# First loads shared by two DMA queues, an early exponential, and one low part moved ahead of two convolution pieces

## The chip, the cores and the metric

The kernel runs on one core of a Trainium2 chip. The metric is device time in microseconds (us): the median over executions of the whole program on that core. The engines are TensorE (PE in the rows, its weight loads PEld), VectorE (DVE), ScalarE (ACT), GpSimd (POOL) and SyncE (SP, which here only issues DMAs). ScalarE can issue DMAs too. A "q" behind an engine's name (SPq, ACTq) marks work of its queue, such as a DMA issue.

## What is computed

Two stages, all in fp32. A dynamic convolution over 7 taps whose weights are a softmax, then a two-layer MLP with a squared ReLU:

```
w = exp(weight_gen - max(weight_gen)); w /= sum(w) + 1e-9       # over the 7 taps, per token and head
out[b,s,h,:] = sum_k w[b,s,h,k] * x_padded[b, s+k, h,:]         # 4 x 4096 tokens, 192 features, 8 heads
h = out @ w_in                                                  # 192 -> 2048
g = s * relu(h)^2 + b
y = g @ w_out                                                   # 2048 -> 192
```

## The kernel before

The 16384 tokens are cut into 32 groups of 512. For each group the convolution runs on VectorE, on a layout of 4 feature quarters by 32 partitions: softmax, four product instructions, five additions, eight 32x32 transposes. The MLP then runs on TensorE in chunks of 128 hidden features. To keep fp32 accuracy from single-pass matmuls, each operand is split into a high part (a rounded copy, made by ScalarE) and a low part (the remainder, made by VectorE or read from a matmul result).

The order of all instructions is written out by hand (`tc.manual_schedule()`): each engine executes its instructions in the order in which the code calls them. The start of the program, about the first 90 us, is special: the weights `w_in` and `w_out` are loaded, split into high and low parts (`convert`), and used for group 0 as they become ready. After that a steady loop of 31 groups runs.

What the change and its surroundings touch, by name:

- `load(i)` loads a group's convolution weights `wg` (four DMAs, one for each feature quarter) and its tokens `xt` (four DMAs). Everything goes through SyncE's queue but for group 0, whose four `xt` DMAs go through ScalarE's.
- `load_weights(k)` loads a quarter of the MLP weights, two `convert` chunks, into the tile `r`: four large DMAs and eight small ones ("tails") of `w_in`, then two of `w_out`, one for each chunk.
- `convert(i)` is a generator of four steps: ScalarE's `Abs` of the loaded chunk (L187, needs the `w_in` DMAs and the chunk's `w_out` DMA); VectorE's L190, L194, L198; the copy to the high part `hi` (L203) with VectorE's L205 and L209; and six matmuls (L219 to L221), whose result ScalarE copies to the low part (L222).
- `run_pieces(g, a, b)` issues pieces a to b-1 of group g's convolution: 0 is the maximum and subtraction (L269, L271), 1 the exponential on ScalarE (L277), 2 the normalisation (L282 to L286), 3 to 6 the products (L300), 7 to 11 the additions (L311, L319), 12 the transposes, 13 and 14 the split into high and low, which end in four DMAs that rearrange the tile `xb` inside the on-chip memory (L355).
- `mm1_pair` (L408, L414) is the first matmul of a chunk, `relu2` (L443, L445, L449) makes `g` and its high part `gh` on ScalarE, `low_g` (L455) its low part `gl` on VectorE, `mm2_pair` (L482) the second matmul.

Each DMA signals its landing on one of eight semaphores, `DMAHW0` to `DMAHW7`. They are given out in turn over both queues, so a DMA waits, before it is issued, for the landing of the DMA eight places ahead of it. A queue that waits holds all that stands behind it.

At the start the code is:

```
load(0, nc.scalar)
constants()
load_weights(0)
load(1)
load_weights(1)
...
run_pieces(0, 0, 2)
ahead(0, 1)
run_pieces(0, 2, 7)
ahead(0, 3)
```

where `ahead(i, n)` issues the next n steps of `convert(i)`. The eight chunks of group 0 follow in a loop over i; in it, `run_pieces(1, *beside[i])` works on group 1's convolution beside them, with pieces 2 and 3 for i = 0.

Of the kernel before, what the change touches and what calls it, by code (L numbers as in the profile page):

```python
# [7 lines left out]
F32 = mybir.dt.float32  # L8
F32R = mybir.dt.float32r
U32 = mybir.dt.uint32  # L10
AF = mybir.ActivationFunctionType
# [9 lines left out]
def dynamic_conv_then_relu2_mlp(  # L21
# [24 lines left out]
    nc = tc.nc  # L46
# [3 lines left out]
    P = 128  # L50
# [39 lines left out]

    ORDER = list(range(1, NG)) + [0]

    def load(i, queue=nc.sync):

        g = ORDER[i]
        xt = xin.tile([P, J + HALO, FQ], F32, tag="x", name="xt")
        wg = xin.tile([P, J, HQ, K], F32, tag="wg", name="wg")
        t0 = g * T
        for q in range(Q):
            p = slice(q * C, (q + 1) * C)  # L100
            nc.sync.dma_start(  # L101
                out=wg[p].rearrange("c j h k -> c j (h k)"),
                in_=wgf[t0:t0 + T, q * HQ * K:(q + 1) * HQ * K].rearrange("(c j) n -> c j n", j=J),
            )
        for q in range(Q):
            p = slice(q * C, (q + 1) * C)
            f = slice(q * FQ, (q + 1) * FQ)
            if g == 0:
                nc.sync.dma_start(
                    out=xt[p, HALO:, :], in_=xf[t0:t0 + T, f].rearrange("(c j) n -> c j n", j=J)  # L110
                )
                for c0, c1 in ((1, C // 2), (C // 2, C)):
                    a = t0 + c0 * J - HALO
                    src = xf[a:a + 1, f]
                    nc.sync.dma_start(
                        out=xt[q * C + c0:q * C + c1, 0:HALO, :],
                        in_=bass.AP(src.tensor, src.offset, [[J * D, c1 - c0], [D, HALO], [1, FQ]]),
                    )
                continue
            src = xf[t0 - HALO:t0 - HALO + 1, f]  # L120
            queue.dma_start(
                out=xt[p],
                in_=bass.AP(src.tensor, src.offset, [[J * D, C], [D, J + HALO], [1, FQ]]),
            )
        xt_t[i], wg_t[i] = xt, wg
# [17 lines left out]
    raw_t = {}  # L143
# [2 lines left out]
    w_in_u = w_in.bitcast(U32)  # L146
    w_out_u = w_out.bitcast(U32)

    def load_weights(k):

        r = raw.tile([P, 2, CW, 2], U32, tag="r", name="r")
        rw = r.rearrange("p c n w -> p c (n w)")
        c0 = k * QUAD * P * 2
        for q in range(Q):
            src = w_in_u[q * FQ:q * FQ + 1, c0:c0 + 1]
            nc.sync.dma_start(
                out=rw[q * 32:(q + 1) * 32, :, CA * 2:CB * 2],
                in_=bass.AP(src.tensor, src.offset, [[F * 2, 32], [2 * P * 2, 2], [1, 2 * P * 2]]),
            )
        for q in range(Q):  # L160
            for i in range(2):
                f = (q + 2 * i) % Q * FQ + 32
                c = c0 + (1 - q // 2) * P * 2
                src = w_in_u[f:f + 1, c:c + 1]
                nc.sync.dma_start(
                    out=rw[q * 32 + i * TAIL:q * 32 + (i + 1) * TAIL, :, CB * 2:CO * 2],
                    in_=bass.AP(src.tensor, src.offset, [[F * 2, TAIL], [2 * P * 2, 2], [1, P * 2]]),
                )
        for c in range(2):
            o = (k * 2 + c) * 2 * P  # L170
            src = w_out_u[o:o + 1, 0:1]
            nc.sync.dma_start(
                out=rw[:, c, CO * 2:].rearrange("p (j n) -> p j n", j=2),
                in_=bass.AP(src.tensor, src.offset, [[D * 2, P], [P * D * 2, 2], [1, D * 2]]),
            )
        raw_t[k] = r

    def convert(i):

# [188 lines left out]
    def run_pieces(g, a, b):  # L368

        if g < NG:  # L370
            if g not in pieces_t:
                pieces_t[g] = conv_pieces(g)
            for f in pieces_t[g][a:b]:
                f()
# [77 lines left out]
    def low_g(n, p):  # L452
        sq, gh = g_t[n, p]
        gl = gp.tile([P, 2, T], F32R, tag="gl", name="gl")
        nc.vector.tensor_tensor(out=gl, in0=sq, in1=gh.bitcast(F32), op=ALU.subtract)  # L455
        g_t[n, p] = gh, gl
# [76 lines left out]

    with tc.manual_schedule():
        load(0, nc.scalar)
        constants()
        load_weights(0)
        load(1)
        load_weights(1)
        nc.sync.dma_start(out=s_sb, in_=s.partition_broadcast(P))  # L540
        nc.sync.dma_start(out=b_sb, in_=b.partition_broadcast(P))

        parts = [convert(i) for i in range(NC)]

        def ahead(i, n):
            for _ in range(n if i < NC else 0):
                next(parts[i])

        run_pieces(0, 0, 2)
        ahead(0, 1)  # L550
        run_pieces(0, 2, 7)
        ahead(0, 3)
        ahead(1, 1)
        run_pieces(0, 7, 15)

        beside = ((2, 4), (4, 5), (5, 7), (7, 8), (8, 10), (10, 12), (12, 14), (14, 15))
        for i in range(NC):
            n, p = divmod(i, 2)
            mm1_pair(n, p)
            if i == 0:  # L560
                ahead(1, 2)
                ahead(2, 1)
            relu2(n, [p], lambda: ahead(i + 1, 1))
            if i == 0:
                run_pieces(1, 0, 2)
            ahead(i + 2, 2)
            ahead(i + 3, 1)
            if i == NC - 1:
                sums = column_sums()
            if i > 0:  # L570
                mm2_pair((i - 1) // 2, (i - 1) % 2)
            run_pieces(1, *beside[i])
            low_g(n, p)
            if i == 0:
                load_weights(2)
            if i == NC - 1:
                set_bias(sums)
            if i == 1:
                load_weights(3)
            if i == 4:  # L580
                load(2)
        run_pieces(2, 0, 3)
        last = NG * NQ - 1
        for n in range(NQ, last + 1):
            g, k = divmod(n, NQ)
            if k == 0 and g + 2 < NG:
                load(g + 2)
            if k == 3:
                zeros_before(g + 2)
            mm1_quad(n)  # L590
            relu2(n)
            if n == NQ:
                mm2_pair(n - 1, 1)
            else:
                mm2_quad(n - 1)
            a = (3, 5), (5, 8), (9, 14), (0, 2)
            run_pieces(g + 1 + k // 3, *a[k])
            low_g(n, 0)
            if k == 0:
                scale(g - 1, (0, 2, 1, 3))  # L600
                store(g - 1, 0, NT)
            low_g(n, 1)
            a = (5, 5), (8, 9), (14, 15), (2, 3)
            run_pieces(g + 1 + k // 3, *a[k])

        for t in range(NT):
            mm2_pair(last, 0, [t], t == NT - 1)
            mm2_pair(last, 1, [t], t == NT - 1)
            scale(NG - 1, [t])
            store(NG - 1, t, t + 1)  # L610
# [30 lines left out]
```

## Time and profile before

| what | us |
|---|---|
| median of 3 executions (1181.53 to 1182.57) | 1181.69 |
| span of the profiled execution, first to last instruction | 1178.3 |
| TensorE busy in it | 1144.9 |
| VectorE busy | 938.2 |
| ScalarE busy | 826.4 |

The profile is of one execution. Its span is 3.4 us shorter than the median: that much of the time lies around the first and the last instruction. All starts below are counted from the span's first instruction.

### The profile page before, as it was taken

How to read it: one execution, taken by the hardware profiler on the slowest of the kernel's cores; microseconds unless marked ns; L12 is line 12 of the kernel's file. 1: busy time of each engine (PE TensorE's matmuls, PEld its weight loads, DVE VectorE, ACT ScalarE, POOL GpSimd, SP SyncE). 2: the span in 40 equal slices, each digit the busy share in tenths (PEclk: the TensorE clock that was granted, in tenths of full speed). 3: DMA queues.
4: the chain of work that ended last, by engine and by line, in shares of the span. 5: the costliest groups of instructions: out<-in, count | busy, mean ns of one | idle time of the engine just before them, and what ended most of it. 6: DMA issues, size and time to landing. Idle time of an engine off the chain costs nothing.

```text
span 1178.3 us, 29855 instructions
## 1 busy us (share of the span) xinstructions
PE 1144.9 (97%) x12672; PEld 1034.5 (88%) x12672; DVE 938.2 (80%) x1357; ACT 826.4 (70%) x889; POOL 6.1 (1%) x22
## 2 busy tenths in 40 slices
PE   2999999999999999999999999999999999999997
PEld 1678999999999999999999999999999999999997
DVE  7988887788887778887778898777788777888843
ACT  2767767777677677776776776767767677677674
POOL 0000000000000000000000000000000000000000
PEclk9999999999999999999999999999999999999999
DMA  7421222221122222122222112222112222212110
GB/s 155 117 44 28 40 46 47 32 46 27 35 46 46 39 40 37 30 40 47 46 33 46 26 36 46 46 35 44 29 37 42 47 46 33 45 26 36 24 24 14
DMA packets 175833, 50.17 MB, mean 43 GB/s; under 512 B 165076, under 2 KB 168660, under 8 KB 175700
## 3 DMA queue, kind: packets, MB, share of 16 engines
q1 hardware_dynamic: 172820, 47.73, 22.6%
q8 instruction: 99, 1.62, 0.6%
q10 hardware_dynamic: 2880, 0.54, 0.3%
q14 instruction: 34, 0.28, 0.1%
HBM read 27.26 MB, written 12.58 MB: 34 GB/s over the span
## 4 chain that ended last, share of the span: by engine, by line
PE 95%; DVE 2%; ACT 1%; DMA 1%; SPq 0%; issue 0%
PE po L500 47%; PE ph L432 43%; PE po L482 2%; PE ph L219 1%; PE ph L408 1%; DVE pr L300 1%; PE ph L414 1%; DMA r<-in_moe_w_in_dram 0%; DVE gl L455 0%; DVE pr L311 0%; ACT gh L449 0%; PE ph L246 0%; ACT r L445 0%; SPq L101 0%; DMA xb<-xb 0%
## 5 line engine op out<-in xcount | busy, mean ns | idle before, releaser
L500 PE MATMUL po<-wc,gh 64*128 64x384 f32 x3936 | 570.5, 356 | 0.0
L500 PE MATMUL po<-wc,gl 64*128 64x192 f32 x3936 | 492.8, 247 | 0.8 <-DVE gl L455 0.8
L455 DVE TENSOR_TENSOR gl<-r,gh 128x1024 fp32r<-128x1024 f32 x256 | 313.1, 1223 | 213.1 <-ACT gh L449 206.9
L443 ACT ACTIVATE r<-ph 128x1024 f32<-128x1024 f32 x256 | 249.0, 1024 | 300.0 <-PE ph L432 295.1
L500 PEld LDWEIGHTS po<-wc,gl 64*128 64x128 f32 x3936 | 375.7, 188 | 6.3 <-DVE gl L455 1.1
L500 PEld LDWEIGHTS po<-wc,gh 64*128 64x128 f32 x3936 | 368.7, 184 | 5.1
L432 PE MATMUL ph<-xa,wc 64*128 64x512 f32 x2976 | 365.6, 391 | 0.0
L432 PEld LDWEIGHTS ph<-xa,wc 64*128 64x128 f32 x2976 | 269.8, 184 | 52.9 <-issue 0.2
L449 ACT CAST gh<-r 128x1024 fp32r<-128x1024 f32 x256 | 269.2, 1052 | 7.9
L445 ACT ACTIVATE r<-r 128x1024 f32<-128x1024 f32 x256 | 270.7, 1057 | 0.3
L300 DVE TENSOR_TENSOR pr<-xt,w 128x1152 f32<-128x1152 f32 (+1 forms) x128 | 193.6, 1554 | 2.5 <-DMA r<-in_moe_w_in_dram 0.7
L432 PE MATMUL ph<-xb,wc 64*128 64x512 f32 x1488 | 190.4, 388 | 0.0
L432 PEld LDWEIGHTS ph<-xb,wc 64*128 64x128 f32 x1488 | 139.9, 184 | 30.5
L311 DVE TENSOR_TENSOR pr<-pr 128x768 f32<-128x768 f32 (+1 forms) x128 | 145.2, 1155 | 2.1
L512 DVE SCALAR_TENSOR_TENSOR u<-po,s_sb,bias 128x192 f32<-128x192 f32 x128 | 49.8, 410 | 1.6 <-PE po L482 1.6
L518 DVE SCALAR_TENSOR_TENSOR y<-po,s_sb,u 128x192 f32<-128x192 f32 x128 | 49.8, 409 | 0.1
L219 PE MATMUL ph<-r,eye_f 128*128 128x384 f32 x32 | 15.6, 570 | 18.2 <-DVE r L198 18.2
L319 DVE TENSOR_TENSOR acc<-pr 128x768 f32<-128x768 f32 x32 | 30.6, 958 | 1.1
L330 DVE STREAM_TRANSPOSE xT<-acc 128x128 f32<-128x128 f32 x128 | 28.5, 280 | 1.1
L335 DVE STREAM_TRANSPOSE xT<-acc 128x128 f32<-128x128 f32 x128 | 27.2, 271 | 0.0
L482 PE MATMUL po<-wc,gh 128*128 128x384 f32 x80 | 23.9, 361 | 0.1
L219 PEld LDWEIGHTS ph<-r,eye_f 128*128 128x128 f32 x32 | 5.7, 205 | 20.8 <-issue 20.8
(45 smaller groups left out, 336.0 us busy)
## 6 DMA issues: line engine op xcount, KB each, us to landing
xt<-in_x_dram SPq DMA_DIRECT2D x120, 132.0 KB, 3.4
out_dram<-y SPq DMA_DIRECT2D x128, 96.0 KB, 1.9
xb<-xb SPq DMA_DIRECT2D x128, 64.0 KB
wg<-in_weight_gen_dram SPq DMA_DIRECT2D x128, 28.0 KB, 2.6
r<-in_moe_w_out_dram SPq DMA_DIRECT2D x8, 384.0 KB, 3.7
r<-in_moe_w_in_dram SPq DMA_DIRECT2D x16, 128.0 KB, 3.0
r<-in_moe_w_in_dram SPq DMA_DIRECT2D x32, 32.0 KB, 2.2
xt<-in_x_dram ACTq DMA_DIRECT2D x4, 132.0 KB, 4.0
```

The lines of the kernel that those rows point to most:

```text
L219: nc.tensor.matmul(out=o, lhsT=eye_f, rhs=fv[:, c], start=True, stop=False)
L300: nc.vector.tensor_tensor(out=pr[:, k0:k1, :, h * G:(h + 1) * G], in0=bass.AP(xs.tensor, xs.offset, [xs.ap[0], [FQ, n], [FQ, J], [1, G]]), ...
L311: nc.vector.tensor_tensor(out=pr[:, o:o + n], in0=pr[:, o:o + n], in1=pr[:, a:a + n], op=ALU.add)
L432: nc.tensor.matmul(out=h_t[n, p][:, j], lhsT=w1(2 * k + p, part, block, j, rows), rhs=v[rows], start=(at < 2 and c == 0), stop=(at >= 4 an ...
L443: nc.scalar.activation(out=r[p], in_=h_t.pop((n, p)), func=AF.Relu)
L445: nc.scalar.activation(out=r[p], in_=r[p], func=AF.Square)
L449: nc.scalar.copy(out=gh, in_=r[p])
L455: nc.vector.tensor_tensor(out=gl, in0=sq, in1=gh.bitcast(F32), op=ALU.subtract)
L482: nc.tensor.matmul(**m)
L500: nc.tensor.matmul(**m)
L512: nc.vector.scalar_tensor_tensor(out=u[i], in0=o_t[g][tiles[i]][:, 1, :], scalar=s_sb, in1=bias, op0=ALU.mult, op1=ALU.add,)
L518: nc.vector.scalar_tensor_tensor(out=y[:, t], in0=o_t[g][t][:, 0, :], scalar=s_sb, in1=u[i - 1], op0=ALU.mult, op1=ALU.add,)
```

## The change

Three things. First, the DMAs of group 0 are shared: quarters 0 and 1 of `wg` and of `xt` go through SyncE's queue, quarters 2 and 3 through ScalarE's, and of the first `load_weights` the second tail of each pair goes through ScalarE's queue, behind group 0's exponential (for this, pieces 0 and 1 are now called ahead of `load_weights(0)`). Second, an exponential of one column of a constant tile is issued on ScalarE right after its first DMAs. Third, for the first chunk (i = 0) `low_g` comes ahead of `run_pieces(1, 2, 4)`.

```
-    def load(i, queue=nc.sync):
+    def load(i, side=nc.sync):
         g = ORDER[i]
+        queues = [nc.sync, nc.sync, side, side]
...
-            nc.sync.dma_start(
+            queues[q].dma_start(
                 out=wg[p].rearrange("c j h k -> c j (h k)"),
...
-            queue.dma_start(
+            queues[q].dma_start(
                 out=xt[p],
...
-    def load_weights(k):
+    def load_weights(k, side=nc.sync):
...
-                nc.sync.dma_start(
+                (nc.sync, side)[i].dma_start(
                     out=rw[q * 32 + i * TAIL:q * 32 + (i + 1) * TAIL, :, CB * 2:CO * 2],
...
         load(0, nc.scalar)
         constants()
-        load_weights(0)
+        warm = const.tile([P, 1], F32, name="warm")
+        nc.scalar.activation(out=warm, in_=ones_f[:, 0:1], func=AF.Exp)
+        run_pieces(0, 0, 2)
+        load_weights(0, nc.scalar)
         load(1)
...
-        run_pieces(0, 0, 2)
         ahead(0, 1)
...
+            if i == 0:
+                low_g(n, p)
             run_pieces(1, *beside[i])
-            low_g(n, p)
+            if i > 0:
+                low_g(n, p)
```

The changed file has one or more lines ahead of these places, so its line numbers are 1 to 6 higher.

On ScalarE, at the start of the program, the rows of the kernel before (with the semaphores that each waits for; `xt` and `wg` are group 0's, `r` the first weights):

```order
L121 DMA xt<-in_x_dram 32x22x48 x2
L121 DMA xt<-in_x_dram 32x22x48 [waits DMAHW1_49]
L121 DMA xt<-in_x_dram 32x22x48 [waits DMAHW4_49]
L277 ACT_TABLE_LOAD
L277 ACTIVATE e<-e 128x224 [waits DVE_49]
L187 ACTIVATE t<-r 128x768 [waits DMAHW4_49,DMAHW5_49,DMAHW3_49,DMAHW6_49,DMAHW2_49,DMAHW7_49,DMAHW1_49,DMAHW0_49]
```

And the same place of the changed kernel:

```order
L102 DMA wg<-in_weight_gen_dram 32x16x14 x2
L122 DMA xt<-in_x_dram 32x22x48 x2
L539 ACT_TABLE_LOAD
L539 ACTIVATE warm<-ones_f 128x1 [waits Pool_49]
L278 ACTIVATE e<-e 128x224 [waits DVE_49]
L167 DMA r<-in_moe_w_in_dram 16x2x256 [waits DMAHW2_49]
L167 DMA r<-in_moe_w_in_dram 16x2x256 [waits DMAHW3_49]
L167 DMA r<-in_moe_w_in_dram 16x2x256 [waits DMAHW5_49]
L167 DMA r<-in_moe_w_in_dram 16x2x256 [waits DMAHW6_49]
L188 ACTIVATE t<-r 128x768 [waits DMAHW4_49,DMAHW5_49,DMAHW3_49,DMAHW6_49,DMAHW2_49,DMAHW7_49,DMAHW1_49,DMAHW0_49]
```

The table load that belongs to the exponential now stands with the early one, none of the first four DMAs waits, and four tails stand behind the exponential.

On SyncE's queue, the start of the program in the kernel before (without the semaphores):

```order
L101 DMA wg<-in_weight_gen_dram 32x16x14 x4
L156 DMA r<-in_moe_w_in_dram 32x2x512 x4
L165 DMA r<-in_moe_w_in_dram 16x2x256 x8
L172 DMA r<-in_moe_w_out_dram 128x2x384 x2
L101 DMA wg<-in_weight_gen_dram 32x16x14 x4
```

And in the changed kernel, with the semaphores. In the order in which they are given out, the two queues alternate over the first eight (ScalarE's `wg`, SyncE's `wg`, and so on: 0 to 3 are `wg`, 4 and 6 ScalarE's `xt`, 5 and 7 SyncE's `xt`):

```order
L102 DMA wg<-in_weight_gen_dram 32x16x14 x2
L122 DMA xt<-in_x_dram 32x22x48 x2
L158 DMA r<-in_moe_w_in_dram 32x2x512 [waits DMAHW0_49]
L158 DMA r<-in_moe_w_in_dram 32x2x512 [waits DMAHW1_49]
L158 DMA r<-in_moe_w_in_dram 32x2x512 [waits DMAHW4_49]
L158 DMA r<-in_moe_w_in_dram 32x2x512 [waits DMAHW7_49]
L167 DMA r<-in_moe_w_in_dram 16x2x256 [waits DMAHW0_49]
L167 DMA r<-in_moe_w_in_dram 16x2x256 [waits DMAHW1_49]
L167 DMA r<-in_moe_w_in_dram 16x2x256 [waits DMAHW2_49]
L167 DMA r<-in_moe_w_in_dram 16x2x256 [waits DMAHW3_49]
L174 DMA r<-in_moe_w_out_dram 128x2x384 [waits DMAHW4_49]
L174 DMA r<-in_moe_w_out_dram 128x2x384 [waits DMAHW5_49]
```

The first `w_out` DMA was the 17th on this queue and is now the 13th. The third and fourth large `w_in` DMAs now stand behind the landing of `xt` DMAs, and the third and fourth tail behind that of ScalarE's first two tails.

On VectorE, around the first `low_g`, in the kernel before (`v` is of convert(2), `sm` to `pr` of group 1's convolution, the `t` behind `gl` of convert(3)):

```order
L209 SCALAR_TENSOR_TENSOR v<-r,t 128x768
L282 TENSOR_REDUCE sm<-e 128x32
L283 TENSOR_SCALAR sm<-sm 128x32
L284 RECIPROCAL sm<-sm 128x32
L286 TENSOR_TENSOR w<-e,sm 128x224
L300 TENSOR_TENSOR pr<-xt,w 128x64x24
L455 TENSOR_TENSOR gl<-r,gh 128x1024
L190 TENSOR_SCALAR t<-t 128x768
```

And in the changed kernel:

```order
L210 SCALAR_TENSOR_TENSOR v<-r,t 128x768
L456 TENSOR_TENSOR gl<-r,gh 128x1024
L283 TENSOR_REDUCE sm<-e 128x32
L284 TENSOR_SCALAR sm<-sm 128x32
L285 RECIPROCAL sm<-sm 128x32
L287 TENSOR_TENSOR w<-e,sm 128x224
L301 TENSOR_TENSOR pr<-xt,w 128x64x24
L191 TENSOR_SCALAR t<-t 128x768
```

`gl` moved ahead of five instructions; nothing else moved on this engine, and nothing at all on TensorE.

## Rows read from the trace of the kernel before

**Rows 1.** The page: the chain that ended last, share of the span by engine.

```profile
PE 95%; DVE 2%; ACT 1%; DMA 1%; SPq 0%; issue 0%
```

**Rows 2.** Stretches: from:to, length, busy us of each engine, granted clock, DMA share, GB/s.

```profile
27.45:31.75 4.30, 2.93 (x6) 1.78 (x6) 4.11 (x6) 0.91 (x2) 0.00 (x0) 1.00 0.38 61
...
41.60:89.70 48.10, 48.10 (x272) 38.50 (x274) 41.79 (x59) 32.43 (x36) 0.00 (x0) 1.00 0.38 83
...
98.70:1150.00 1051.30, 1051.29 (x12064) 960.35 (x12066) 847.12 (x1223) 757.31 (x813) 5.31 (x16) 1.00 0.22 38
```

**Rows 3.** Chain that ended last, in order of time: start, us, what.

```profile
29.34 2.31 DMA xb<-xb
...
35.83 1.05 ACT gh L449
```

**Rows 4.** Timeline of the first 16.5 us: start, us, engine, line [idle before, releaser].

```profile
0.81 5.42 ACTq L121 DMA_DIRECT2D xt<-in_x_dram  x4
...
0.81 2.74 SPq L101 DMA_DIRECT2D wg<-in_weight_gen_dram  x4
...
6.01 0.39 DVE L269 TENSOR_REDUCE mx<-wg 128x32 f32<-128x224 f32 x1 [4.19 <-DMA wg<-in_weight_gen_dram]
6.26 1.28 ACT L277 ACT_TABLE_LOAD   x1 [6.26 <-DMA wg<-in_weight_gen_dram]
...
7.55 0.39 ACT L277 ACTIVATE e<-e 128x224 f32<-128x224 f32 x1
...
9.00 0.39 DVE L286 TENSOR_TENSOR w<-e,sm 128x224 f32<-128x224 f32 x1
10.12 5.96 DVE L300 TENSOR_TENSOR pr<-xt,w 128x1536 f32<-128x1536 f32 x4 [0.73 <-DMA r<-in_moe_w_in_dram]
10.17 0.94 SPq L172 DMA_DIRECT2D r<-in_moe_w_out_dram  x2
...
13.56 0.91 ACT L187 ACTIVATE t<-r 128x768 f32<-128x768 f32 x1 [5.62 <-DMA r<-in_moe_w_out_dram]
...
16.00 0.55 DVE L190 TENSOR_SCALAR t<-t 128x768 f32<-128x768 f32 x1
```

**Rows 5.** DMA issues in narrow windows: count, KB, us from issue to landing.

```profile
wg<-in_weight_gen_dram SPq DMA_DIRECT2D x1, 28.0 KB, 3.5
...
xt<-in_x_dram SPq DMA_DIRECT2D x4, 132.0 KB, 3.3
...
r<-in_moe_w_out_dram SPq DMA_DIRECT2D x1, 384.0 KB, 3.1
```

**Rows 6.** DMA packets: `wg` (q1, 3.5:4.2) and `xt` (q10, 2.9:3.5), share of 16 engines.

```profile
q1 hardware_dynamic: 912, 0.05, 92.0%
...
q10 hardware_dynamic: 532, 0.10, 98.9%
```

**Rows 7.** Timeline of SyncE's queue: eight tails of the second weights.

```profile
18.43 3.78 SPq L165 DMA_DIRECT2D r<-in_moe_w_in_dram  x8
```

**Rows 8.** Timeline around the first `low_g`, VectorE and TensorE.

```profile
37.20 0.39 DVE L282 TENSOR_REDUCE sm<-e 128x32 f32<-128x224 f32 x1 [0.58 <-ACT e L277]
...
41.60 0.36 PE L482 MATMUL po<-wc,gl 128*128 128x192 f32 x1 [0.86 <-DVE gl L455]
```

**Rows 9.** VectorE from there to the third `low_g`, and TensorE behind it.

```profile
37.20:55.46 18.26, 17.40 (x88) 12.54 (x87) 17.70 (x22) 14.68 (x17) 0.00 (x0) 1.00 0.41 114
...
54.24 1.22 DVE L455 TENSOR_TENSOR gl<-r,gh 128x1024 fp32r<-128x1024 f32 x1
...
55.52 0.36 PE L482 MATMUL po<-wc,gl 128*128 128x192 f32 x1
```

**Rows 10.** Stretch 10 to 11 us, columns as in group 2.

```profile
10.00:11.00 1.00, 0.00 (x0) 0.00 (x0) 0.88 (x1) 0.00 (x0) 0.00 (x0) 1.00 0.21 65
```

**Rows 11.** Timeline of TensorE: the first matmuls of chunk 0 and of chunk 2.

```profile
27.52 2.93 PE L408 MATMUL ph<-xa,wc 128*128 128x512 f32 x6 [5.10 <-ACT xa L342]
...
43.80 1.58 PE L408 MATMUL ph<-xa,wc 128*128 128x512 f32 x6
```

More of the change, by code (lines that the diff above doesn't have):

```diff
@@ L147, in dynamic_conv_then_relu2_mlp @@
     w_out_u = w_out.bitcast(U32)
-    def load_weights(k):
+    def load_weights(k, side=nc.sync):
         r = raw.tile([P, 2, CW, 2], U32, tag="r", name="r")
+        raw_t[k] = r
         rw = r.rearrange("p c n w -> p c (n w)")
@@ L175, in load_weights @@
             )
-        raw_t[k] = r
     def convert(i):
```

## The prediction

> **What bounds the kernel now.** I start with the chain that ended last: TensorE holds 95% of it, VectorE, ScalarE and the transfers the rest [rows 1]. Next, the stretches: from 98.7 to 1150 us TensorE is busy 1051.29 of 1051.30 us, and from 41.6 to 89.7 us 48.10 of 48.10 [rows 2]. The change touches neither TensorE's order nor its work, so from 41.6 us on it can only let that work begin earlier. What there is to win lies ahead of 41.6 us, and the question is which wait there ends last.
>
> Read back from 41.6 us. TensorE sat idle 0.86 us until the first low part `gl` was ready [rows 8]. Its `gh` had ended at 35.83 + 1.05 = 36.88 us [rows 3]; `gl` stood behind five VectorE instructions. `gh` itself hangs on TensorE's work that began when the rearranged `xb` landed at 29.34 + 2.31 = 31.65 us [rows 3]. `xb` is the end of group 0's convolution on VectorE, which from 16.00 us on, at convert(0)'s first instruction, runs in its written order with hardly a gap. Ahead of it stand the four products, 10.12 to 16.08 us, and ahead of those 0.73 us of idle time [rows 4]. The row names a weight DMA as its end, but the products read only `xt` and `w`; `w` was done at 9.00 + 0.39 = 9.39 us, so the late one is `xt`, whose last DMA left ScalarE's queue only at 0.81 + 5.42 = 6.23 us, since it waited for a `wg` DMA's semaphore; it landed some 3.9 us later.
>
> So every step of the chain from the start to 31.65 us moves with one instruction: VectorE's first of convert(0), at 16.00 us. It needs two things: VectorE done with the products, and ScalarE's Abs, which started at 13.56 us on the landing of the first `w_out` DMA and took 0.91 us, to 14.47 us [rows 4]. In the kernel before the products decide, with 1.5 us to spare. I work out both anew.
>
> **The products.** The second `wg` DMA of each queue is issued at about 1.6 us, as SyncE's second was: four took 2.74 us from 0.81 us on, the first a little more than the rest [rows 4]. That one took 3.5 us to land, with ScalarE's `xt` packets beside it [rows 5]; the last, issued near 2.9 us with little beside it, some 3.0 us, as the maximum started on it at 6.01 us [rows 4]. Now only `wg` is beside it, so I take 3.0: all `wg` has landed at 4.6 us, against some 5.9 us. The maximum starts 0.1 us later, at 4.7 us. From its start to the exponential's start took 7.55 - 6.01 = 1.54 us before, with the table load of 1.28 us from 6.26 to 7.54 us in between; without that wait the exponential follows the subtraction, 0.85 us after the maximum's start. The table load now runs from about 3.2 to 4.5 us, behind four DMA issues and while ScalarE has nothing to do, and the early exponential of one column (between nothing and the 0.39 us of the 224-column one) hides there too. From the exponential's start to the end of `w` it is 9.39 - 7.55 = 1.84 us [rows 4]. So `w` is ready at 4.7 + 0.85 + 1.84 = 7.4 us.
>
> `xt`: 912 `wg` packets filled 92.0% of 0.7 us, so four `wg` DMAs of 512 packets are 1.45 us of all 16 engines; 532 `xt` packets filled 98.9% of 0.6 us, so four of 704 are 3.14 us [rows 6]. Behind `wg`, landed at 4.6 us, 3.14 us of `xt` end at 7.7 us; some `xt` packets will get in ahead of the last of `wg`, and I take 7.5 us for the landing. The low bound is the last issue, at about 2.95 us, plus 3.0 us (four on one queue had a median of 3.3 [rows 5]): 6.0 us. The high bound, with weight packets in between, is 8.0 us. I stay near the upper one, since the engines are full there. The products start at 7.6 and end at 13.55 us.
>
> **The first weights.** SyncE now issues `wg` and `xt` ahead of the weights. Its fourth large `w_in` DMA waits for SyncE's own second `xt`, until 7.5 us. Behind it stand four tails; eight took 3.78 us [rows 7], 0.47 us each. So the first `w_out` DMA is issued at 7.5 + 5 x 0.47 = 9.8 us, against 10.17 us [rows 4]: four places fewer ahead of it, but behind a new wait. It lands 3.1 us later [rows 5], at 12.9 us; Abs starts 0.3 us behind that, as before (10.17 + 3.1 against 13.56), and ends at 14.1 us. VectorE's first instruction of convert(0) starts at 14.15 us, not at 13.55 us: the weights, not the products, are now late. **First term: 16.00 - 14.15 = 1.85 us.** Bounds: with `xt` at 6.0 us the third large `w_in`, issued near 5.2 us, still has to land (3.1 us) before `w_out` is issued at 8.3 us, Abs ends at 12.6 us, and the products, behind `w` at 7.4 us, decide at 13.4 us: 2.6 us. With `xt` at 8.0 us and a further 0.6 us lost to ScalarE's tails, which stand behind the exponential and must land before SyncE's last two tails are issued, `w_out` goes at 10.9 us: 0.75 us.
>
> Nothing else is issued in another place. SyncE's later DMAs keep their order and end no later than before if `w_out` is not later; the rearranging DMAs, now wanted near 25.6 us, find the queue free: eight tails ended at 22.2 us [rows 7], and two `w_out` (0.94 us) and two small DMAs behind them end near 24.2 us.
>
> **The earlier low part.** VectorE sat idle 0.58 us, from 36.62 to 37.20 us, until group 1's exponential was ready [rows 8]. `gl` can fill that from 36.90 us, when `gh` is done. It frees TensorE's 0.86 us at once. But those 0.86 us are not all kept: from 37.20 us to the end of the third `gl` at 55.46 us VectorE runs without a wait (17.70 busy of 18.26 us, the rest being gaps between dependent instructions), and TensorE took that `gl` at 55.52 us, 0.06 us behind its end [rows 9]. Two iterations on, VectorE is the one that is waited for. Its own row of work only starts 37.20 - 36.90 = 0.30 us earlier. **Second term: 0.30 us**, bounded by 0 and 0.86.
>
> **The sum.** 1.85 + 0.30 = 2.15 us off the span of 1178.3 us, and, what lies around the span being the same, 1181.69 - 2.15 = **1179.5 us**. The bounds give 1181.69 - 3.46 = 1178.2 and 1181.69 - 0.75 = 1180.9. This is 0.18%, and 0.2% (2.36 us) is about what a measurement tells from no change: the forecast lies just inside.
>
> **Rivals.**
>
> *The loads are no sooner* (1179.9 us, up to no change). Two queues issue, but the 16 engines carry the same bytes. If they set the pace, `w_out` lands as before, Abs ends at 14.47 us, and the first term is 1.5 us; with the second 1.8 us. Against: from 10 to 11 us, just when `w_out` is issued, the engines were 21% busy [rows 10], so issue and semaphores had held it, not the engines. For: the new waits of SyncE's queue. If `wg` landed at 5.9 us as before, ScalarE's second tail would go out near 7.8 us, land 3.9 us later, as the late `xt` did, and `w_out` would go near 11.9 us: no gain from the first term.
> The Trainium skill (DMA: Bandwidth & Descriptors, section Issuing engines are not separate DMA queues) says that DMAs of all issuing engines run on the same 16 and that issuing from several saves only the sequencer's time. By that rule the sum would be this rival's 1.8 us. The 21% speaks against it for `w_out`; the packets of `wg` and `xt` [rows 6] agree with it, and I have used them so.
>
> *The weights are early enough* (1178.8 us, 1178.2 at most). The first term becomes 2.6 us, with 0.30 us 2.9 us. For: the transfers of the first microseconds were timed while competing with others. Against: the engine time of `xt` above.
>
> *Slower* (1187.6 us). The first matmuls of chunk 0 took 2.93 us for six where the same six took 1.58 us later [rows 11], though the granted clock of that stretch is 1.00, the 2.4 GHz level [rows 2]. If with earlier work the slow form lasted until 40.74 us, where TensorE met its wait, its work behind `xb` would double: 3.3 us ahead of `gh` (31.65 to 35.83 us, less a ScalarE copy of some 0.8 us) and 4.8 us behind it. 8.1 - 2.15 = 5.9 us later. It decides once more than 2.15 us is added. Against: all of TensorE's work ahead moves by the same amount, so its distances stay.
>
> **Chances.** My forecast, 1179.1 to 1180.0 us, 0.43; no sooner 0.22; early enough 0.30; slower 0.05. Faster by over 0.2% is below 1179.33 us: the third case and a third of the first, 0.43 in all. Slower by over 0.2% 0.04; the same 0.53. The range reaches from the early case's end to the late one's, 1178.1 to 1181.1 us.
>
> **What would show it.** Right: the table load near 3.3 us; the maximum near 4.7, the products near 7.6 us; ScalarE's Abs ending after the products, near 14.1 us, and a wait of some 0.6 us of VectorE on it; `gl` directly behind `v`; TensorE without its 0.86 us, but with a wait at the second or third `gl`. Wrong: Abs done before the products end (early weights), `w_out` issued after 10.2 us (late ones), no wait of TensorE at the third `gl` (the second term then nears 0.86), or slow matmuls behind 31.65 - 1.85 us.

## The result, and the profile after

| what | before | after |
|---|---|---|
| median of 5 executions, us | 1181.53 (1179.94 to 1182.57) | 1189.77 (1188.12 to 1189.97) |
| ratio, 95% interval | | 1.0067 (1.0056 to 1.0079) |
| span of the profiled execution | 1178.3 | 1186.4 |
| TensorE busy in it | 1144.9 | 1153.1 |

The change costs 8.2 us. TensorE's busy time grew by the same 8.2 us, although its instructions and their order are the same. The profiled execution of the changed kernel took 1188.12 us, 1.7 us more than its span, and in every run this difference is 1.7 to 1.8 us; the profiled execution of the kernel before was thus one of its faster ones, near 1180.0 us, and 1.7 us lie around its span, not the 3.4 us given above. The line numbers of the changed kernel are 1 higher around TensorE's work (L433 is L432 of before, L501 is L500).

The chain of the changed kernel by engine, from the page; it answers to [rows 1].

```profile
PE 94%; DVE 3%; DMA 1%; ACT 1%; SPq 0%; issue 0%; DVEq 0%
```

The same bound as before. The stretch of the steady loop after, which answers to the last of [rows 2] (the columns are those):

```profile
98.70:1150.00 1051.30, 1051.30 (x11972) 952.84 (x11971) 843.78 (x1220) 750.74 (x807) 5.30 (x16) 1.00 0.23 38
```

TensorE is as busy as before and its granted clock is the same 1.00, but it gets through 11972 matmuls where it was 12064. At 1051.3 us for 12064, the 92 that are missing are 92 x 87.1 ns = 8.0 us. So the loss is not at the start, where the change is, but in the matmuls of the loop.

The chain in the loop shows which. First two steps of the kernel before (start, length, what):

```profile
303.35 4.16 PE ph L432 x36
307.51 4.56 PE po L500 x64
312.07 4.16 PE ph L432 x36
316.23 4.56 PE po L500 x64
```

And of the changed kernel:

```profile
304.58 4.22 PE ph L433 x36
308.80 4.57 PE po L501 x64
313.37 4.22 PE ph L433 x36
317.59 4.57 PE po L501 x64
```

One step is 36 first-layer matmuls (`ph`, L432, streaming `xa` and `xb`) and 64 second-layer ones (`po`). The first block grew from 4.16 to 4.22 us, the second hardly. Taken more finely, as the mean over the 90 to 92 blocks that lie whole between 300 and 1100 us, from the start of a block's first matmul to that of the next block: 4156.7 to 4221.7 ns, and 4563.3 to 4565.0 ns. These means are called "the block" and "the second block" below. The page counts 2976 + 1488 matmuls of the first kind after, which is 124 blocks; 124 x 65.0 ns + 123 x 1.7 ns = 8.3 us. The loop alone makes the loss.

The instructions of the first layer that stream `xa`, between 98.7 and 1150 us, before (shapes, count | busy us, mean ns of one | idle before):

```profile
L432 PE MATMUL ph<-xa,wc 64*128 64x512 f32 x2890 | 355.0, 391 | 0.0
L432 PEld LDWEIGHTS ph<-xa,wc 64*128 64x128 f32 x2892 | 262.0, 184 | 51.1
```

And after:

```profile
L433 PE MATMUL ph<-xa,wc 64*128 64x512 f32 x2874 | 358.1, 394 | 0.0
L433 PEld LDWEIGHTS ph<-xa,wc 64*128 64x128 f32 x2876 | 260.3, 184 | 55.2
```

The weight load takes 184 ns in both; the matmul itself takes 394 instead of 391 ns, with nothing waited for.

The start of the changed kernel, its timeline of the first 16.5 us, answers to [rows 4]:

```profile
3.45 1.28 ACT L539 ACT_TABLE_LOAD   x1 [3.45 <-issue]
3.73 4.84 SPq L158 DMA_DIRECT2D r<-in_moe_w_in_dram  x4
...
4.94 0.39 DVE L270 TENSOR_REDUCE mx<-wg 128x32 f32<-128x224 f32 x1 [3.12 <-DMA wg<-in_weight_gen_dram]
...
7.23 0.39 DVE L287 TENSOR_TENSOR w<-e,sm 128x224 f32<-128x224 f32 x1
8.37 5.97 DVE L301 TENSOR_TENSOR pr<-xt,w 128x1536 f32<-128x1536 f32 x4 [0.74 <-DMA xt<-in_x_dram]
8.91 2.36 SPq L167 DMA_DIRECT2D r<-in_moe_w_in_dram  x4
11.31 0.94 SPq L174 DMA_DIRECT2D r<-in_moe_w_out_dram  x2
...
14.93 0.89 ACT L188 ACTIVATE t<-r 128x768 f32<-128x768 f32 x1 [8.75 <-DMA r<-in_moe_w_out_dram]
...
15.85 0.56 DVE L191 TENSOR_SCALAR t<-t 128x768 f32<-128x768 f32 x1 [1.51 <-ACT t L188]
```

The softmax is early, as the change means it to be: `w` is done at 7.62 us instead of 9.39. The weights are not: the first `w_out` DMA is issued at 11.31 us instead of 10.17, and convert(0) starts at 15.85 us, 0.15 us sooner than before.

The chain in these microseconds names what holds `w_out`:

```profile
5.79 4.68 DMA r<-in_moe_w_in_dram
...
10.49 0.31 SPq L167
...
10.85 0.42 SPq L167
...
11.31 0.42 SPq L174
```

A tail that ScalarE issued at 5.79 us took 4.68 us to land, and SyncE's third tail waited for it until 10.49 us. Two tails later `w_out` could go.

Further on, the last DMA of `xb` and the first `gh` in the chain answer to [rows 3]; the first `gl`, which starts directly behind that `gh`, is a row of VectorE's timeline:

```profile
29.19 2.42 DMA xb<-xb
...
35.79 1.06 ACT gh L450
```

```profile
36.87 1.23 DVE L456 TENSOR_TENSOR gl<-r,gh 128x1024 fp32r<-128x1024 f32 x1 [0.41 <-ACT gh L450]
```

VectorE's third `gl`, and TensorE behind the second and the third, answer to [rows 9]:

```profile
53.91 1.22 DVE L456 TENSOR_TENSOR gl<-r,gh 128x1024 fp32r<-128x1024 f32 x1
```

```profile
47.80 0.36 PE L483 MATMUL po<-wc,gl 128*128 128x192 f32 x1 [0.27 <-DVE gl L456]
...
55.19 0.36 PE L483 MATMUL po<-wc,gl 128*128 128x192 f32 x1 [0.29 <-DVE gl L456]
```

TensorE no longer idles 0.86 us ahead of the first `gl`, but 0.27 us ahead of the second and 0.29 us ahead of the third; there it is 55.52 - 55.19 = 0.33 us ahead of the kernel before. The chain's first long block of the loop starts at 98.41 us, 0.31 us sooner than the 98.72 us of before. That is all that the change gained.

### The profile page after: what moved, and what is told of

Read it like the earlier page. It is cut to its first block, busy times and chain, and to the rows that moved or that the text cites. A ratio compares the mean times of both kernels' runs of the same rounds, so it can differ in the third digit from the quotient of the medians.

```text
span 1186.4 us, 29857 instructions
## 1 busy us (share of the span) xinstructions
PE 1153.1 (97%) x12672; PEld 1034.2 (87%) x12672; DVE 938.3 (79%) x1357; ACT 826.1 (70%) x890; POOL 6.1 (1%) x22
## 4 chain that ended last, share of the span: by engine, by line
PE 94%; DVE 3%; DMA 1%; ACT 1%; SPq 0%; issue 0%; DVEq 0%
PE po L501 47%; PE ph L433 44%; PE po L483 1%; DVE gl L456 1%; PE ph L220 1%; DMA wg<-in_weight_gen_dram 1%; DVE pr L301 1%; PE ph L409 0%; DMA r<-in_moe_w_in_dram 0%; PE ph L415 0%; DVE pr L312 0%; ACT gh L450 0%; PE ph L247 0%; DVE r L199 0%; ACT r L446 0%
## 5 line engine op out<-in xcount | busy, mean ns | idle before, releaser
L501 PE MATMUL po<-wc,gh 64*128 64x384 f32 x3936 | 570.8, 356 | 0.0
L501 PE MATMUL po<-wc,gl 64*128 64x192 f32 x3936 | 493.5, 247 | 0.7 <-DVE gl L456 0.7
L501 PEld LDWEIGHTS po<-wc,gl 64*128 64x128 f32 x3936 | 375.7, 188 | 6.2 <-DVE gl L456 1.0
L501 PEld LDWEIGHTS po<-wc,gh 64*128 64x128 f32 x3936 | 369.1, 184 | 5.5
L433 PE MATMUL ph<-xa,wc 64*128 64x512 f32 x2976 | 371.0, 394 | 0.0
L433 PEld LDWEIGHTS ph<-xa,wc 64*128 64x128 f32 x2976 | 269.6, 184 | 57.3 <-issue 0.2
L433 PE MATMUL ph<-xb,wc 64*128 64x512 f32 x1488 | 193.0, 391 | 0.0
L433 PEld LDWEIGHTS ph<-xb,wc 64*128 64x128 f32 x1488 | 139.5, 184 | 34.1
```

The source lines that it names most:

```text
L433: nc.tensor.matmul(out=h_t[n, p][:, j], lhsT=w1(2 * k + p, part, block, j, rows), rhs=v[rows], start=(at < 2 and c == 0), stop=(at >= 4 an ...
L501: nc.tensor.matmul(**m)
```

## The experiments

In every program the tiles of a pool lie behind those of the pool allocated before it. The only thing in the change that moves tiles is `warm`, a new tile of one fp32 column: in the built program it takes 32 bytes of each partition at the end of the pool `const`, and every tile of the pools behind it, `xa` and `xb` too, begins 32 bytes further on. The converted weights `wc` were placed ahead of it and stay. The theory was that these 32 bytes slow TensorE's loop; its rivals were the moved `low_g` and the new order of the loads. Where a range stands behind it or a number of executions is given, a time is a median, compared with the kernel before on the same chip; every other time is of one execution. Executions of one kernel differ by some 2 us, so single times are read together with the block.

**Which part of the change.** The changed kernel with a larger `warm`:

```
-        warm = const.tile([P, 1], F32, name="warm")
-        nc.scalar.activation(out=warm, in_=ones_f[:, 0:1], func=AF.Exp)
+        warm = const.tile([P, 16], F32, name="warm")
+        nc.scalar.activation(out=warm[:, 0:1], in_=ones_f[:, 0:1], func=AF.Exp)
```

> The changed kernel, with the early exponential's tile made 16 columns wide (64 bytes in each partition) in place of one (which takes 32); only column 0 is written, as before. Theory A, addresses: the 32 bytes moved every tile placed behind the constants from a multiple of 64 bytes to 32 beyond one, and TensorE reads such tiles more slowly; with 64 bytes they are back on multiples of 64, the 36 first matmuls of a loop step take 4.16 us again and not 4.22, and the time is 0.3 us under the kernel before (1181.2 where that is 1181.5). Theory B, timing: the loop is slower because the new start brings the engines or the transfers into another rhythm; the block stays at 4.22 us and the time at 1189 to 1190.

Measured: 1186.58 us (1186.08 to 1188.42), ratio 1.0044 (1.0031 to 1.0056); block 4205.8 ns, second block 4574.2. The place changes the time, but 64 bytes do not restore it: that part of the theory, that a multiple of 64 is what counts, fell.

The kernel before with nothing but an unused tile of the same size:

```
+        pad = const.tile([P, 1], F32, name="pad")
+        nc.gpsimd.memset(pad, 0.0)
```

> The kernel before, with one more constant tile of one column (32 bytes in each partition), filled once by GpSimd at the start; nothing else changes. Theory A, addresses: the block of 36 first matmuls takes 4.22 us in place of 4.16, some 8 us in all: 1189.5 us. Theory B, timing of the new start: nothing changes, 1181.5 us.

Measured: 1191.02 us (1190.34 to 1191.26), ratio 1.0078 (1.0064 to 1.0092); block 4221.7 ns, as in the changed kernel. Of the change this kernel has only the 32 bytes, and it has the whole loss.

The kernel before with the moved `low_g` alone:

```
+            if i == 0:
+                low_g(n, p)
             run_pieces(1, *beside[i])
-            low_g(n, p)
+            if i > 0:
+                low_g(n, p)
```

> The kernel before with the earlier low part alone. Both theories: the block of 36 stays at 4.16 us. The prediction's second term: VectorE's third low part ends 0.30 us earlier, the steady loop begins 0.3 us earlier, 1181.2 where the kernel before is 1181.5; if VectorE did not bind two steps on, 0.86 us.

Measured: 1181.64 us over 11 executions, ratio 0.9998 (0.9990 to 1.0007); block 4156.7 ns. In its profile the loop's first long block starts at 98.49 us, 0.23 us sooner than before; in the time such a gain can't be told from nothing.

The other two parts, with the 64-byte `warm` and `low_g` back in its old place:

```
-            if i == 0:
-                low_g(n, p)
             run_pieces(1, *beside[i])
-            if i > 0:
-                low_g(n, p)
+            low_g(n, p)
```

> The changed kernel with the 64-byte tile and with the low part at its old place: the shared loads and the early exponential alone. Theory A: the block of 36 takes 4.16 us, and the time is that of the kernel before within 0.1 us, since the first term measured next to nothing (the first instruction of convert(0) 0.15 us earlier). Theory B: 4.22 us, 1189 to 1190.

Measured: 1188.19 us (1186.75 to 1189.00), ratio 1.0053 (1.0040 to 1.0065); block 4205.8 ns as in the first. `low_g` has no part in the loss.

The whole change without the new tile; the early exponential writes into a column of `bias`, which VectorE fills later:

```
-        warm = const.tile([P, 1], F32, name="warm")
-        nc.scalar.activation(out=warm, in_=ones_f[:, 0:1], func=AF.Exp)
+        nc.scalar.activation(out=bias[:, 0:1], in_=ones_f[:, 0:1], func=AF.Exp)
```

> The changed kernel with the early exponential written into a column of the tile bias, which is filled much later, so that no new tile is placed and every tile stands at the address of the kernel before. Theory A, addresses: the block of 36 first matmuls takes 4.16 us, the block of 64 second ones 4.56, and the time is 0.3 us under the kernel before, within what can be measured of it. Theory B, something else in the changed start slows the loop: 4.21 us or more, 1187 or more.

Measured: 1181.37 us over 11 executions against 1181.80, ratio 0.9998 (0.9989 to 1.0007); block 4156.6 ns. Without the 32 bytes the change costs nothing, and what it gains is too small to be told from nothing.

**Which tiles.** The kernel before with the pool of `xa` and `xb` allocated last, so that it can be moved alone:

```
-    xtp = ctx.enter_context(tc.tile_pool(name="xtp", bufs=2))
...
     yp = ctx.enter_context(tc.tile_pool(name="yp", bufs=2))
+    xtp = ctx.enter_context(tc.tile_pool(name="xtp", bufs=2))
```

> The kernel before with the pool of xa and xb placed last in place of ahead of the pools of r, g and y; no tile's place changes modulo 2048 bytes. A control for the next two: if only the place within 2048 bytes counts, the blocks stay at 4.16 and 4.56 us, and 1180 to 1182 us in all.

Measured: 1181.71 us, block 4156.6 ns. Then 32 unused bytes ahead of that pool:

```
+    padp = ctx.enter_context(tc.tile_pool(name="padp", bufs=1))
+    padp.tile([P, 8], F32, name="pad2")
     xtp = ctx.enter_context(tc.tile_pool(name="xtp", bufs=2))
```

> As the control, with 32 unused bytes ahead of the last pool: only xa and xb, which TensorE streams in the first matmuls, move by 32 bytes. Theory A1, the streamed operand's address counts: the block of 36 takes 4.22 us. Theory A2, the address of the other tiles counts (gh and gl, loaded as weights, or the tiles that ScalarE and VectorE work on): 4.16 us.

Measured: 1188.34 us. A block of its chain in the loop:

```profile
306.24 4.22 PE ph L434 x36
```

Last, the reverse: 32 bytes in `const`, and 2016 ahead of the last pool, so that `xa` and `xb` move by 2048 bytes and all others behind `const` by 32.

```
+    const.tile([P, 1], F32, name="pad")
...
+    padp = ctx.enter_context(tc.tile_pool(name="padp", bufs=1))
+    padp.tile([P, 504], F32, name="pad2")
```

> As the control, with 32 unused bytes behind the constants and 2016 ahead of the last pool: every tile moves by 32 bytes but xa and xb, which keep their place modulo 2048. Theory A1: the block of 36 takes 4.16 us. Theory A2: 4.22 us.

Measured: 1182.83 us, the block 4158.3 ns:

```profile
305.94 4.16 PE ph L435 x36
```

So it is `xa` and `xb`, what the first layer streams, and not the other tiles that the 32 bytes moved: moved alone, `xa` and `xb` give 60.9 of the 65.0 ns, the others under 2 ns.

**Which places.** The pad of the kernel with 32 bytes, with other sizes; only `xa` and `xb` move.

> An unused 128-byte pad is allocated ahead of the last pool, so only the input tiles xa and xb lie 128 bytes further on than in the kernel before with that pool last (whose block of 36 first-layer matmuls took 4156.6 ns; with the pad at 32 bytes 4217.5). Theory short period: the places repeat with 128 bytes, so the block is as with no pad, 4157 ns, and the time as before, within 1.2 us of 1181. Theory long period: they repeat with 256 bytes or more, so the block is 4200 to 4225 ns and the time 1186 to 1189 us.

> As the 128-byte pad, with 256 bytes. Theory short period (128 bytes) and theory of 256 bytes: block of 4157 ns, 1180 to 1182.5 us. Theory of a longer period (1024 or 2048 bytes, or a fixed place in relation to the weights): 4200 to 4225 ns, 1186 to 1189 us.

> As the 128-byte pad, with 1024 bytes. Every theory of a period of up to 1024 bytes: block of 4157 ns and 1180 to 1182.5 us. A period of 2048 bytes or a place that counts in relation to the other operand: 4200 to 4225 ns, 1186 to 1189 us.

> As the 128-byte pad, with 64 bytes, so that xa and xb begin at a multiple of 256 bytes. Theory one good place: of the eight places in 256 bytes only that of the kernel before gives 4157 ns to the block; here 4200 to 4225 ns, 1186 to 1189 us (with all tiles moved by 64 bytes it was 4206 ns). Rival, several places with values of their own: with xa and xb alone at a multiple of 256 bytes the block is at most 4157 ns, and the 4206 ns came of the other tiles.

> As the 128-byte pad, with 96 bytes. Theory one good place: 4200 to 4225 ns, 1186 to 1189 us. Rival, several places: a value of its own, down to the 4068 ns that the block would take if each of its 18 pairs took the 226 ns of the shortest in the kernel before, and a time lower by 0.123 us for each ns that the block loses.

> As the pad of 96 bytes, with 160 bytes. Theory one good place: 4200 to 4225 ns, 1186 to 1189 us. Rival, several places: a value of its own, 4157 ns or less.

> As the pad of 96 bytes, with 192 bytes, so that xa and xb begin at an odd multiple of 128 bytes. Theory one good place: 4200 to 4225 ns, 1186 to 1189 us. Rival, several places: a value of its own, 4157 ns or less.

Measured, one execution each; the last column is a block's length over 36, the mean time from matmul to matmul:

| pad, bytes | time, us | block, ns | ns a matmul |
|---|---|---|---|
| 0 | 1181.71 | 4156.6 | 115.5 |
| 32 | 1188.34 | 4217.5 | 117.2 |
| 64 | 1187.74 | 4203.3 | 116.8 |
| 96 | 1187.86 | 4233.3 | 117.6 |
| 128 | 1186.32 | 4217.5 | 117.2 |
| 160 | 1188.98 | 4219.2 | 117.2 |
| 192 | 1176.61 | 4115.0 | 114.3 |
| 256 | 1179.89 | 4156.7 | 115.5 |
| 1024 | 1182.31 | 4156.7 | 115.5 |

Pads of 256 and 1024 bytes count like none, so the period is 256 bytes or a part of it, and the 128-byte pad rules out 128. One good place in 256 bytes was wrong: a pad of 192 bytes is better than both kernels. The kernel before stood at the second best of the seven places tried, and the change moved it to one of the five poor ones. The eighth, 224, was not tried. A block of the best:

```profile
312.55 4.12 PE ph L434 x36
```

**The place itself, or the relation to the weights.** At the pad of 192 bytes `xa`, `xb` and the weights `wc` all begin at an odd multiple of 128 bytes in the built program. The weight tiles had not moved in any kernel so far. Now both move:

```
+    const.tile([P, 32], F32, name="pad3")
     wc = [const.tile([P, 2, CW], F32R, name=f"wc_{i}") for i in range(NC)]
...
+    padp.tile([P, 48], F32, name="pad2")
```

> The kernel with the 192-byte pad, with another 128 bytes unused ahead of the weight tiles, so that weights and xa, xb both move by 128 bytes and begin at multiples of 256 bytes. Theory of the place itself: xa and xb count as with the 64-byte pad, where they also began at a multiple of 256 bytes, block 4203 ns, 1186 to 1188 us. Theory of the relation to the weights: it is unchanged from the 192-byte pad, block 4115 ns, 1175 to 1177 us.

Measured: 1174.91 us, block 4115.0 ns.

```profile
310.87 4.12 PE ph L435 x36
```

`xa` and `xb` stand here at a multiple of 256 bytes, as with the 64-byte pad, where the block took 4203.3 ns; the weights now stand 128 bytes from where they stood there. So it is not the place of the streamed tile but its distance from the weight tile that counts, modulo 256 bytes. Shown is this for one distance (0) at two places. All other tiles moved along by 128 bytes here, but in the kernels above their place made little difference: 1.7 ns when they moved by 32 bytes alone, 4.2 ns (4221.7 against 4217.5) and 2.5 ns (4205.8 against 4203.3) when they moved with `xa` and `xb` by 32 and by 64.

**The best of both.** The changed kernel without its new tile, and with `xa` and `xb` allocated last behind a pad of 192 bytes:

```
-        warm = const.tile([P, 1], F32, name="warm")
-        nc.scalar.activation(out=warm, in_=ones_f[:, 0:1], func=AF.Exp)
+        nc.scalar.activation(out=bias[:, 0:1], in_=ones_f[:, 0:1], func=AF.Exp)
...
+    padp.tile([P, 48], F32, name="pad2")
+    xtp = ctx.enter_context(tc.tile_pool(name="xtp", bufs=2))
```

> The changed kernel without its new tile (the early exponential writes into a column of bias), with the pool of xa and xb allocated last, 192 bytes further on. Theory place: the block of 36 is 4115 ns as with the 192-byte pad alone, 41.6 ns under the 4156.6 of the kernel before, and 123 loop steps times that are 5.1 us, so the median is 1176.0 to 1177.0, the ratio to before 0.9957 with an interval below 0.998. Rival, the gain belonged to that one run (its granted clock rose at another moment) and goes with a timed comparison: 1180.5 to 1182, ratio 0.999 to 1.0005.

Measured: 1175.96 us (1174.77 to 1176.84) against 1180.61, ratio 0.9957 (0.9944 to 0.9971); block 4115.0 ns. It is 4.7 us faster than the kernel before, where the changed kernel was 8.2 us slower.

**Why the weights came late.** The changed kernel without its new tile, and with all tails on SyncE's queue:

```
-        load_weights(0, nc.scalar)
+        load_weights(0)
```

> The changed kernel with no new tile (the early exponential writes into a column of bias, which the block's loads fill later), and all eight weight tails back on SyncE's queue; ScalarE keeps its w_gate and x transfers. Theory order: the changed kernel's w_out is late because SyncE's third tail waits for ScalarE's tail, which took 4.68 us to land; with all tails on SyncE they wait for the x transfer and the four w_in transfers instead, w_out is issued at about 12.0 us (11.31 in the changed kernel), the absolute values end at about 16.5 and SyncE's convert starts at 16.6, 0.7 us later than in the changed kernel. Rival, transfers set the pace: the DMA engines need the same time for the same bytes, w_out lands at the same 14.9 us and the conversion starts at 15.85. The time itself is 1181 to 1182.5 us in both.

Measured: 1180.93 us. Both theories missed. Its chain:

```profile
5.31 5.17 DMA r<-in_moe_w_in_dram
...
10.49 0.31 SPq L167
...
10.84 0.42 SPq L174
```

`w_out` goes at 10.84 us, sooner than the 11.31 of the changed kernel (11.15 without its tile), and convert(0) starts at 15.16 us instead of 15.85 (15.62). The last wait is now on the fourth large `w_in` DMA, issued at 5.31 us, and it ends at the same 10.49 us as the wait for ScalarE's tail in the changed kernel (10.33 without its tile). What this DMA had beside it shows in the busy share of the transfer engines in 40 slices of the first 15 us (0.375 us each), before:

```profile
DMA  0000049999947699999999953432219899789999
```

And after:

```profile
DMA  0000005944999999999999999996402117989999
```

In the changed kernel the engines are 90% busy or more without a break from 3.8 to 10.1 us; before they were that from 2.3 to 4.1 and from 5.3 to 8.6 us. This fits a start in which the first loads and weights land as fast as the engines carry them, near 10.4 us, and what is left after that is the number of issues still ahead of `w_out`: two tails in the changed kernel, one in this one. It is argued, not shown: no run changes the bytes of these loads alone. Shared tails cost 0.31 us here (11.15 - 10.84), not the 0.7 us in the other direction that the first theory gave them; these are single executions, and the changed kernel with and without its tile, whose start is the same, differ by 0.16 us.

## Why the prediction was wrong

The time, 1189.77 us, lies 8.7 us above the upper end of the range, and on the side that had a chance of 0.04.

**The step that failed** is in the first paragraph: "The change touches neither TensorE's order nor its work, so from 41.6 us on it can only let that work begin earlier." Order and work did stay, but in this kernel a matmul's time did not follow from these alone: the 32 bytes of `warm` moved the tiles that the loop streams, and each of 124 blocks took 65 ns more. The prediction priced the early exponential by its ScalarE time and never by its tile. The experiments show this cause from both sides: 32 unused bytes in the kernel before give the whole loss (1191.02 us), the change without them gives none (1181.37 us). Why the distance of the two operands counts is not shown.

**The rival "slower"** named another mechanism, first-layer matmuls in the slow form up to 40.74 us, and a time of 1187.6 us. The time came near by chance, the mechanism did not occur: the loss is in the loop, and the loop starts sooner than before. The granted clock of 1.00 that this rival read for the slow matmuls is no measured clock: the trace of the kernel before has no clock record before 31.2 us, and the views count such a stretch as 1.00. In the last section the same six matmuls take the same 2.93 us where a record says 0.51, so the slow form was the lower clock, 1.2 GHz. It ended ahead of `xb`'s first matmuls in both kernels (their records begin with 1.00 at 31.2 us before, at 30.3 us after).

**First term, 1.85 us; measured 0.15 us** at VectorE's first instruction of convert(0), and 0.04 us at the landing of `xb` (29.19 + 2.42 = 31.61 instead of 31.65 us). The softmax took as long as worked out, 0.2 us later (the maximum at 4.94 instead of 4.7 us, `w` at 7.62 instead of 7.4). `xt` landed near 8.3 us, outside its bound of 8.0 by a little, and the products ended at 14.34 instead of 13.55 us. The weights decided, as the forecast said, and VectorE waited 1.51 us for them instead of some 0.6; but `w_out` went at 11.31 instead of 9.8 us, later than the bound of 10.9. The 0.6 us that the bound gave to ScalarE's tails was the real path, and the tail took 4.68 us to land in engines that were full; `w_out` itself then took 3.6 us to the start of Abs instead of 3.4. In the forecast transfers were priced by rows from less crowded moments.

The rival "the loads are no sooner" was right in its outcome for this term, "no gain from the first term", and not in its path. It had ScalarE's second tail go out near 7.8 us, because `wg` would land at 5.9 us as before; `wg` had landed by 4.94 us, ScalarE's first tail went out at 5.79 us, and the loss was in its landing. The rival's time for `w_out`, near 11.9 us, was 0.6 us off, the late bound's 10.9 us 0.4 us. Its first form, `w_out` as before and 1.8 us in all, did not come: `w_out` went 1.14 us later than before. The rule of the Trainium skill that went with it (DMA: Bandwidth & Descriptors, section Issuing engines are not separate DMA queues) says that issuing from a second engine saves only issue time. The trace agrees: the transfer engines stayed at 90% or more until 10.1 us.

**Second term, 0.30 us; measured 0.30 us.** VectorE's row of work starts with `gl` at 36.87 us instead of 37.20 us [rows 8], 0.33 us sooner. Of this, 0.03 us is an earlier `gh` (35.79 + 1.06 = 36.85 instead of 36.88 us), which is what was left of the first term; 0.30 us is the order. The reasoning held: TensorE's 0.86 us went away and came back as waits at the second and third `gl`, and the third `gl` starts the same 0.33 us sooner (53.91 instead of 54.24 us).

**Both terms** together were to give 2.15 us and gave 0.31 us at the start of the loop. Taken off 1181.69 us this is 1181.4 us, just above the range's end of 1181.1; the kernel without the tile took 1181.37 us (ratio 0.9989 to 1.0007, that is 1.3 us less to 0.8 more). So even without the tile the time would have been outside the range, by 0.3 us, for what the first term fell short.

## What to carry to other kernels

A new tile is not free because nothing waits for it: it moves all tiles allocated behind it, and in a kernel that is bound by matmuls of the same form over and over, some per cent of their time can hang on where the streamed tile lies in relation to the weights. So when a change adds, removes or resizes a tile, look first at the mean time of one steady matmul before and after; if it differs while order and count don't, put the tile elsewhere (behind the others, or into an existing one) before judging the change. And since places differ, a few pads tried on purpose are a cheap experiment: here one of them took 41.6 ns off each of 124 blocks, 5.2 us, where the change's edits gained 0.31 us in the trace.

## What was not expected of the hardware

- The same matmul takes 114.3 to 117.6 ns from start to start (block over 36) by the distance between the streamed tile and the weight tile modulo 256 bytes, while the weight load stays at 184 to 185 ns. The Trainium skill (TensorE: Matmul & The Clock Gate, section Step-by-step: what each phase is for) says that TensorE reads the streamed operand and the weights through two independent ports, so that a weight load takes no bandwidth from the running matmul. The measurement does not fit two operands that are without effect on each other: with the weights moved by 128 bytes the same place of `xa` and `xb` gave 4115.0 instead of 4203.3 ns a block. Whether the ports are where they meet, no run here shows.
- The second layer hardly minded: its block stayed within 4553.3 and 4574.2 ns in all kernels. Its operands `gh` and `gl` were moved in relation to the weights by 32 and 64 bytes only.
- Executions of one and the same kernel differ by some 2 us. Part of it is the clock at the start. Of 15 executions of the kernel before on one chip, the three with a mean granted clock of 1.000 took 1179.81 to 1179.95 us, the twelve with 0.995 to 0.998 took 1181.45 to 1182.31 us. From 25.3 to 35.5 us the kernel with the pool last, below it the one with both operands moved, and the changed kernel without its tile (columns as in [rows 2]):

```profile
25.30:35.50 10.20, 6.74 (x17) 4.36 (x18) 9.50 (x21) 5.04 (x6) 0.00 (x0) 0.51 0.25 55
```

```profile
25.30:35.50 10.20, 6.46 (x21) 3.99 (x21) 9.60 (x21) 5.54 (x7) 0.00 (x0) 1.00 0.18 34
```

```profile
25.30:35.50 10.20, 6.95 (x17) 4.56 (x18) 9.49 (x20) 5.12 (x6) 0.00 (x0) 1.00 0.30 71
```

The granted clock of the first is 0.51, near the 1.2 GHz level. The 1.00 of the other two must not be read as the 2.4 GHz level: their traces have no clock record before 30.5 and 36.7 us, where one with 1.00 begins, and a stretch without a record counts as 1.00. The matmuls show the clock. The first two groups of six first-layer matmuls in the first of these kernels:

```profile
27.36 2.93 PE L408 MATMUL ph<-xa,wc 128*128 128x512 f32 x6 [5.15 <-ACT xa L342]
...
31.69 1.74 PE L414 MATMUL ph<-xb,wc 64*128 64x512 f32 x6 [1.40 <-DMA xb<-xb]
```

And in the second:

```profile
27.48 2.93 PE L411 MATMUL ph<-xa,wc 128*128 128x512 f32 x6 [5.10 <-ACT xa L345]
...
31.74 1.06 PE L417 MATMUL ph<-xb,wc 64*128 64x512 f32 x6 [1.33 <-DMA xb<-xb]
```

Up to 30.5 us both are equally slow. Then the clock of the second rises while TensorE waits for `xb`, and that of the first stays low until 35.7 us. TensorE's work ahead was the same: 5.1 us idle, six matmuls, 1.3 to 1.4 us idle. The first long block of the loop starts at 100.36 us in the first and at 98.48 us in the second, although the instructions ahead of it are the same. What sets which of the two an execution gets was not found out.
